# Output stores through two queues, and a finer table of stages for the schedule, in an attention and two-MoE kernel

## The chip, the cores and the metric

The kernel runs on one core of a Trainium2 chip. The metric is the device time of one execution in microseconds (us). TensorE (PE) multiplies matrices, with a sequencer of its own for the loads of the stationary operand (PEld); VectorE (DVE), ScalarE (ACT) and GpSimd (POOL) work on elements; SyncE (SP) issues transfers to the core's 16 DMA engines. Each engine runs its instructions in the order in which the program has them.

## The reference

Three parts follow each other; all data are fp32.

```python
# attention, B4 H8 S768 D64: local window of 96 and 8 global keys, ALiBi bias
a = softmax(where(keep, q @ k.T / 8 - slope * dist, -1e9)); x = a @ v     # -> x (3072, 512)
# first layer, 512 -> 1024 -> 512
h = x @ w_in; s = h * softmax(h); x = layernorm(s) * g_ln @ w_out
# soft MoE: 32 slots, 8 experts of 512 -> 1024 -> 512
logits = x @ phi                                   # (3072, 32)
d = softmax(logits, axis=0); slots = d.T @ x       # over the tokens
slots = relu(slots @ w1[e]) @ w2[e]                # 4 slots for each expert e
out = softmax(logits, axis=1) @ slots              # (3072, 512)
```

The softmax over the tokens and the slot inputs need every token, so nothing of the experts can be computed before the last token tile is through the first layer.

## The kernel before, in words

The 3072 tokens are 24 tiles of 128. For each tile `att_load` (line 555) loads q, k and v, `att_quad` (565) does the attention of four heads, `x_out` (639) makes the tile's x in two parts, and `moe` (649) does the first layer: two groups of twelve 128x512 matmuls, one for each half of the 1024 columns, a maximum of each half on DVE, the exponent of each half on ACT, the product on DVE, and the layernorm. Tiles are taken in pairs by `slots_of` (730): transposes and logits, `l4` (the logits, 32 slots by 256 tokens), matmuls with the constant `sel4` that give the logits by slot and by token, a running maximum and sum by slot, the exponents for the slots (`l4` again) and for the tokens (`c_all`), and the update of `acc`, the weighted sum of the tokens. The last two tiles (22 and 23) are taken singly; tile 23 has its logits from `last_logits` (705) and its layernorm from `bn_stats`. Then `slot_inputs` (811) makes the 32 slot inputs, `hidden` (841, stage `up`) and `slot_outputs` (867, stages `down0` and `down1`) run the experts over 32 weight tiles of 1 MB (`next_wx`, 800), and `combine` (917, stages `out0` and `out1`) makes the output, once for each half of 256 columns: six groups `g4` of four token tiles, each of four matmuls into two PSUM banks, an ACT copy for the first bank, a DVE copy for the second, and one store of 512 KB whose rows in memory are 256 floats (1 KB) long.

Nothing of this is issued in the order of the code. The class `Plan` records every instruction with a stage name, the one that was set last by `self.stage(...)`. `order` (273) sorts them by a list schedule: an instruction's priority is the length of the longest path behind it plus the offset of its stage from the table `AHEAD` (69 to 71); `schedule` (226) takes, from the instructions that can start within `look` ns, the one of highest priority, and lets `PE` keep the shape of its array unless another instruction is ahead by `STAY`. The best of six rounds by the planner's own clock is taken, and `issue` (287 on) writes the instructions out in that order; line 297 stands for all of them in the profile. So the table decides the order on every engine, and each engine then runs in that order.

The buffers' names in the orders and the profile: `b_61` to `b_68` are the PSUM banks b0 to b7, `s_...` parts of the 25 slots in SBUF, `acc`, `c_all`, `l_69` (`l4`), `sel_75` (`sel4`) and `small` as above; a number behind a name is the buffer's. Profile rows leave the numbers out.

Of the kernel before, what the change touches and what calls it, by code (L numbers as in the profile page):

```python
# [57 lines left out]
class Plan:  # L58
# [7 lines left out]
        ("ACT", "ACT"): 130, ("ACT", "DVE"): 140, ("ACT", "PE"): 160, ("ACT", "POOL"): 160,  # L66
        ("POOL", "POOL"): 104, ("POOL", "PE"): 135, ("POOL", "DVE"): 80, ("POOL", "ACT"): 150,
    }
    TURN, STAY, DEEP = 68, 1362, 240
    WRITES = ("out", "accum_out")  # L70
    AHEAD = {"att": -720, "conv": -1209974, "ct": 295072, "down0": 1163900, "down1": -340751, "init": -242959, "load": -1228290, "logits": -521737, "moe": -630, "out0": 2023604, "out1": 496991, "slots": 82, "sums": -2292290, "tab": 2166439, "tail": 2777910, "up": -870817, "w": 865355, "w2": 249441}

    def __init__(self, nc):
        self.nc = nc
# [195 lines left out]
                    waiting[ops[i]["eng"]].append(i)  # L270
        return start, fin, nth

    def order(self, rounds=6, look=121):
        n = len(self.ops)
        pred = [o["pred"] for o in self.ops]
        back = [{} for _ in range(n)]
        for i in range(n):
            for j, lag in pred[i].items():
                back[j][i] = lag
        tail = [0.0] * n  # L280
        for i in reversed(range(n)):
            tail[i] = self.ops[i]["ns"] + max((lag + tail[k] for k, lag in back[i].items()), default=0.0)
        prio = [-x - self.AHEAD.get(o["stage"][0], 0) for x, o in zip(tail, self.ops)]
        best = None
        for _ in range(rounds):
            start, fin, nth = self.schedule(pred, prio, look, True)
            if best is None or max(fin) < best[0]:
                best = (max(fin), start, nth)
            prio = [-x for x in self.schedule(back, [-x for x in fin], look)[1]]
        self.end, start, nth = best  # L290
        return sorted(range(n), key=lambda i: (start[i], nth[i]))
# [28 lines left out]
class Build:  # L320
# [244 lines left out]
    def att_quad(self, t, hq):  # L565

        self.stage("att", t)
        nc = self.nc
        first = t % NQB == 0
        n, m = P if first else WIN, WIN - P  # L570
        x = self.qkv[t]
        v = x[:, 4 * QK:4 * QK + 512]
        pr = self.pr_ring()[:, 0:4 * WIN].rearrange("p (h n) -> p h n", h=4)
        st = self.att_st()
        ps = [self.bank(SC + j) for j in range(2)]
        qk = x[:, 2 * hq * QK:2 * hq * QK + 2 * QK]
        if t < SPLIT:
            parts = [(qk, qk)]
        else:
            hi, lo = f32r(self.qk_ring()), f32r(self.qk_ring())  # L580
            if hq:
                nc.vector.tensor_copy(out=hi, in_=qk)
            else:
                nc.scalar.copy(out=hi, in_=qk)
            nc.gpsimd.tensor_tensor(out=lo, in0=qk, in1=f32v(hi), op=ALU.subtract)
            parts = [(hi, hi), (hi, lo), (lo, hi)]
        for i2 in range(2):
            q = i2 * QK
            with self.together():
                for i, (a, b) in enumerate(parts):  # L590
                    for j in range(2):
                        r = slice(64 * j, 64 * j + 64)
                        nc.tensor.matmul(out=ps[j][:, 256 * i2:256 * i2 + n], lhsT=a[r, q:q + P], rhs=b[r, q + P:q + P + n],
                                         start=(i == 0), stop=(i == len(parts) - 1))
        for h in range(4):
            i2, j = divmod(h, 2)
            nc.vector.tensor_tensor_reduce(
                out=pr[:, h, 0:n], in0=ps[j][:, 256 * i2:256 * i2 + n], in1=self.tabs[first][:, 4 * hq + h, :], scale=-0.125,
                scalar=3.0e38, op0=ALU.add, op1=ALU.min, accum_out=st[:, h:h + 1],
            )  # L600
        for h in range(4):
            nc.scalar.activation(out=pr[:, h, 0:n], in_=pr[:, h, 0:n], func=AF.Exp, bias=st[:, h:h + 1], scale=-1.0,
                                 accum_out=st[:, 8 + 2 * h:9 + 2 * h])
        share = st[:, 4:8]
        nc.vector.tensor_reduce(out=share, in_=st[:, 8:16].rearrange("p (h c) -> p h c", c=2), axis=AX.X, op=ALU.add)
        nc.vector.reciprocal(out=share, in_=share)
        tr = []
        for i2 in range(2):
            w = pr[:, 2 * i2:2 * i2 + 2]
            nc.gpsimd.tensor_tensor(out=w[:, :, 0:n], in0=w[:, :, 0:n],  # L610
                                    in1=share[:, 2 * i2:2 * i2 + 2].unsqueeze(2).to_broadcast([P, 2, n]), op=ALU.mult)
            pt = self.t_ring().rearrange("p (c n) -> p c n", c=4)
            ptT = self.pt_ring().rearrange("p (c n) -> p c n", c=4)
            tr.append(ptT)
            with self.together():
                for j in range(2):
                    nc.tensor.transpose(pt[:, j, :], w[:, j, 0:P], self.ident)
                if not first:
                    for j in range(2):
                        nc.tensor.transpose(pt[0:m, 2 + j, :], w[:, j, P:WIN], self.ident)  # L620
            nc.scalar.copy(out=ptT[:, 0:2, :], in_=pt[:, 0:2, :])
            if not first:
                nc.scalar.copy(out=ptT[0:m, 2:4, :], in_=pt[0:m, 2:4, :])
        av = self.bank(AV).rearrange("p (c n) -> p c n", c=4)
        for i2 in range(2):
            hp, ptT = 2 * hq + i2, tr[i2]
            with self.together():
                for j in range(2):
                    h = 2 * hp + j
                    nc.tensor.matmul(out=av[64 * j:64 * j + 64, hp, :], lhsT=v[:, h * D:(h + 1) * D], rhs=ptT[:, j, :],  # L630
                                     start=True, stop=first)
                if not first:
                    vt = self.vt[t]
                    for j in range(2):
                        h = 2 * hp + j
                        nc.tensor.matmul(out=av[64 * j:64 * j + 64, hp, :], lhsT=vt[0:m, h * D:(h + 1) * D],
                                         rhs=ptT[0:m, 2 + j, :], start=False, stop=True)

    def x_out(self, t):
        nc = self.nc  # L640
        x = self.x_views[t % (2 * NX)]
        xh, xl = f32r(x[:, 0:512]), f32r(x[:, 512:1024])
        av = self.bank(AV)
        nc.scalar.copy(out=xh, in_=av)
        nc.vector.tensor_tensor(out=xl, in0=av, in1=f32v(xh), op=ALU.subtract)
        self.x[t] = (xh, xl)


    def moe(self, u):
# [20 lines left out]
        for half in range(2):  # L670
            o = slice(half * 512, half * 512 + 512)
            nc.scalar.activation(out=ex[:, o], in_=hs[half], func=AF.Exp, bias=st[:, 2:3], scale=1.0,
                                 accum_out=st[:, 4 + half:5 + half])
            nc.vector.scalar_tensor_tensor(out=z[:, o], in0=hs[half], scalar=1.0, in1=ex[:, o], op0=ALU.mult,
                                           op1=ALU.mult, accum_out=st[:, 6 + half:7 + half])
            if last:
                nc.vector.bn_stats(out=self.bn[:, half, :], in_=z[:, o])
        nc.vector.tensor_reduce(out=st[:, 8:10], in_=st[:, 4:8].rearrange("p (a b) -> p a b", a=2), axis=AX.X, op=ALU.add)
        nc.vector.tensor_scalar(out=st[:, 3:4], in0=st[:, 9:10], scalar1=-1.0 / DFF, scalar2=None, op0=ALU.mult)
        scaled, eps = st[:, 10:11], st[:, 12:13]  # L680
# [48 lines left out]

    def slots_of(self, *us):  # L730

        self.stage("slots", us[0])
        nc = self.nc
        k = len(us)
        zs = [self.z.pop(u) for u in us]
# [6 lines left out]
        else:  # L742
            pl = pd = self.ld_bank(us[0])
            by_slot, by_token = pl[:, 256:256 + k * P], pl[:, 0:k * NS].rearrange("p (k s) -> p k s", k=k)
            for i, z in enumerate(zs):
# [8 lines left out]
                with self.together():  # L754
                    for r in range(2):
                        for g in range(4):
                            nc.tensor.matmul(out=pl[32 * g:32 * g + 32, i * P:(i + 1) * P], lhsT=self.w2[:, r * 4 + g, :],
                                             rhs=zt[:, r * 4 + g, :], start=(r == 0), stop=(r == 1), tile_position=(0, 32 * g))
            nc.vector.tensor_copy(out=l4, in_=pl[:, 0:k * P])
            with self.together():  # L760
                nc.tensor.matmul(out=by_slot, lhsT=self.sel4, rhs=l4, start=True, stop=True)
# [22 lines left out]
        with self.together():  # L784
            for i in range(k):
                nc.tensor.transpose(pd[:, 256 + i * P:256 + (i + 1) * P], dT[:, i * P:(i + 1) * P], self.ident)
        nc.vector.tensor_copy(out=d, in_=pd[:, 256:256 + k * P].rearrange("p (k n) -> p k n", k=k)[:, :, 0:NS])
        with self.together():
            for i, z in enumerate(zs):
# [127 lines left out]
    def combine(self, half, sc):  # L917
        nc = self.nc
        self.stage("out%d" % half)
        for g4 in range(6):  # L920
            o = self.o_ring()
            for pair in range(2):
# [6 lines left out]
                    nc.vector.tensor_copy(out=dst, in_=ps)  # L929
                else:  # L930
                    nc.scalar.copy(out=dst, in_=ps)
            nc.sync.dma_start(
                out=self.out[g4 * 512:(g4 + 1) * 512, half * 256:half * 256 + 256].rearrange("(i p) e -> p i e", p=P),
                in_=o.rearrange("p (i e) -> p i e", i=4),
            )
# [291 lines left out]
```

## Time and profile before

| | us |
|---|---|
| median of 3 runs | 434.69 (434.65 to 435.98) |
| profiled execution | 434.6 |
| its span | 432.9 |

| engine | busy us | share | instructions |
|---|---|---|---|
| PE | 396.7 | 92% | 3595 |
| PEld | 294.8 | 68% | 3595 |
| DVE | 321.6 | 74% | 1209 |
| ACT | 308.8 | 71% | 952 |
| POOL | 187.5 | 43% | 180 |

The span runs from the first to the last event of the execution; the time is a little longer, by what lies around it. A share is a mean over stages: PE is full for most of the span, but not at its end. The trace gives, besides, the stretches in which each engine is full, what an engine waited for, and the instructions in order of time.

### The profile page before, as it was taken

Reading aid. Unit: us, or ns where it says so; the run is one execution under the profiler, and the core shown is the slowest. Engines: PE = TensorE matmul, PEld = TensorE weight load, DVE = VectorE, ACT = ScalarE, POOL = GpSimd, SP = SyncE. Lnnn points to the kernel's source line nnn. Section 1 sums busy time; section 2 is a strip of 40 time slices with the busy share of each in tenths; the row PEclk is TensorE's granted clock in tenths of the full one; section 3 lists DMA queues with packets and bytes.
Section 4 is the critical chain, followed back from the end, with each engine's and each line's share of the span. In section 5 each row is a group of like instructions: output and inputs, shape, how many; then the busy total and the mean of one; then the engine's idle time right before and its main releaser. Section 6 shows DMA issues by size and latency. Waiting matters only on the chain.

```text
span 432.9 us, 10268 instructions
## 1 busy us (share of the span) xinstructions
PE 396.7 (92%) x3595; PEld 294.8 (68%) x3595; DVE 321.6 (74%) x1209; ACT 308.8 (71%) x952; POOL 187.5 (43%) x180
## 2 busy tenths in 40 slices
PE   1898999999999999999999999999999998899960
PEld 0555666778888878887887887878877876334540
DVE  6889897989888888888887888987577879301360
ACT  4899999988888788987988788888546555211240
POOL 1679878675563555735555466372100004100000
PEclk9999999999999999999999999999999999999995
DMA  7983767193312332212331213214320599999597
GB/s 280 345 270 126 277 241 246 48 359 137 117 35 84 117 116 95 79 48 109 117 117 48 90 75 118 94 46 188 160 97 2 201 366 338 397 405 423 230 339 227
DMA packets 20139, 78.01 MB, mean 180 GB/s; under 512 B 2480, under 2 KB 8624, under 8 KB 15984
## 3 DMA queue, kind: packets, MB, share of 16 engines
q1 hardware_dynamic: 20080, 77.28, 48.7%
q8 instruction: 30, 0.49, 0.5%
q14 instruction: 29, 0.24, 0.2%
HBM read 70.98 MB, written 6.29 MB: 179 GB/s over the span
## 4 chain that ended last, share of the span: by engine, by line
PE 80%; ACT 6%; DVE 6%; POOL 2%; DMA 2%; issue 1%; SPq 0%; DVEq 0%; POOLq 0%; ACTq 0%
PE b L297 80%; ACT s L297 6%; DVE s L297 3%; DVE small L297 2%; POOL s L297 2%; DMA s<-in_qkv_dram 2%; DVE l L297 1%; SPq L297 0%; DVE acc L297 0%; DVE small L383 0%; DVE small L381 0%; DVE small L382 0%; DVE small L384 0%; DVE small L379 0%; DVEq L297 0%
## 5 line engine op out<-in xcount | busy, mean ns | idle before, releaser
L297 PE MATMUL b<-s,s 128*128 128x512 f32 (+3 forms) x1568 | 235.0, 347 | 2.7 <-DVE s L297 1.8
L297 PEld LDWEIGHTS b<-s,s 128*128 128x128 f32 (+3 forms) x1568 | 149.4, 153 | 42.9 <-issue 11.1
L297 ACT ACTIVATE s<-s,small 128x240 f32<-128x240 f32 (+2 forms) x215 | 117.7, 555 | 13.4 <-DVE small L297 13.3
L297 ACT COPY s<-b 128x256 f32<-128x256 f32 (+1 forms) x244 | 94.9, 438 | 36.2 <-PE b L297 34.6
L297 POOL TENSOR_TENSOR s<-s,s 128x736 fp32r<-128x736 f32 (+2 forms) x56 | 90.2, 1615 | 61.9 <-ACT s L297 30.5
L297 POOL TENSOR_TENSOR s<-s,small 128x480 f32<-128x480 f32 (+1 forms) x96 | 89.7, 954 | 60.6 <-DVE small L297 39.3
L297 PE MATMUL b<-ident,s 128*128 128x128 f32 (+1 forms) x600 | 90.8, 279 | 5.6 <-ACT s L297 3.2
L297 PEld LDWEIGHTS b<-ident,s 128*128 128x128 f32 (+1 forms) x600 | 69.2, 140 | 28.7 <-issue 9.2
L297 DVE TENSOR_SCALAR small<-small 128x1 f32<-128x1 f32 (+2 forms) x289 | 60.1, 215 | 13.4 <-ACT s L297 6.0
L297 DVE CUSTOM_DVE_ANT_0 s<-b,s 128x240 f32<-128x240 f32 (+1 forms) x192 | 64.5, 382 | 4.9 <-PE b L297 4.4
L297 PE MATMUL b<-s 64*128 64x240 f32 (+2 forms) x528 | 52.1, 320 | 11.1 <-DMA s<-in_qkv_dram 9.3
L297 PEld LDWEIGHTS b<-s 64*128 64x128 f32 (+1 forms) x528 | 39.2, 194 | 23.9 <-DMA s<-in_qkv_dram 9.3
L297 DVE TENSOR_REDUCE small<-b 128x1 f32<-128x512 f32 (+3 forms) x73 | 39.0, 557 | 7.1 <-PE b L297 5.7
L297 ACT ACTIVATION_READ_ACCUMULATOR s<-s,small 128x1 f32 x215 | 42.9, 200 | 0.0
L297 ACT ACTIVATE s<-b,small 128x512 f32<-128x512 f32 x49 | 33.5, 689 | 9.3 <-DVE small L297 7.8
L297 DVE SCALAR_TENSOR_TENSOR s<-b,s 128x512 f32<-128x512 f32 x48 | 32.3, 689 | 7.4 <-ACT s L297 4.1
L297 DVE COPY s<-b 128x512 f32<-128x512 f32 (+1 forms) x20 | 12.3, 635 | 23.6 <-PE b L297 23.3
L297 ACT CAST s<-b 128x512 fp32r<-128x512 f32 (+1 forms) x32 | 18.5, 579 | 15.7 <-PE b L297 15.6
L297 PE MATMUL b<-s,l 128*32 128x256 f32 (+1 forms) x320 | 27.4, 469 | 1.2 <-DVE l L297 0.9
L297 POOL CAST s<-c_all 128x256 fp32r<-128x256 f32 x6 | 2.4, 396 | 58.6 <-DVE s L297 55.1
L297 DVE TENSOR_REDUCE small<-small 128x4 f32<-128x8 f32 (+2 forms) x96 | 14.8, 154 | 13.4 <-ACT s L297 12.1
L297 ACT ACTIVATE s<-s 128x512 f32<-128x512 f32 (+1 forms) x32 | 21.3, 691 | 2.8 <-DMA s<-in_w_in_dram 2.8
(82 smaller groups left out, 292.7 us busy)
## 6 DMA issues: line engine op xcount, KB each, us to landing
s<-in_wx_dram SPq DMA_DIRECT2D x32, 1024.0 KB, 7.7
s<-in_qkv_dram SPq DMA_DIRECT2D x24, 992.0 KB, 5.1
out_dram<-s SPq DMA_DIRECT2D x12, 512.0 KB, 5.5
s<-in_v_tail_dram SPq DMA_DIRECT2D x20, 224.0 KB, 5.2
s<-in_w_in_dram SPq DMA_DIRECT2D x8, 512.0 KB, 4.8
s<-in_w_out_dram SPq DMA_DIRECT2D x8, 512.0 KB, 4.0
acc<-in_phi_dram SPq DMA_DIRECT2D x1, 64.0 KB, 4.9
small<-in_n_dram SPq DMA_DIRECT2D x1, 2.0 KB, 2.7
```

Source lines behind the costliest of these rows:

```text
L297: f(*(self.now(x, age) for x in a), **{k: self.now(x, age) for k, x in kw.items()})
```

## The change

The transfers of `combine` go alternately to SP (even `g4`) and POOL (odd `g4`), the table of offsets is new, with more stages in it, and `STAY` and `look` have other values. New stage names split `att` (`qk`, `soft`, `norm`, `turn`, `av`), `x_out` (`x`), the tail of `moe` (`ln`) and `slots_of` (`zt`, `slots`, `dz`). No instruction is added or removed.

```diff
-    TURN, STAY, DEEP = 68, 1362, 240
+    TURN, STAY, DEEP = 68, 1443, 240
-    AHEAD = {"att": -720, "conv": -1209974, "ct": 295072, "down0": 1163900, "down1": -340751, "init": -242959, "load": -1228290, "logits": -521737, "moe": -630, "out0": 2023604, "out1": 496991, "slots": 82, "sums": -2292290, "tab": 2166439, "tail": 2777910, "up": -870817, "w": 865355, "w2": 249441}
+    AHEAD = {"att": 336137, "av": -663, "conv": -1209818, "ct": 563852, "down0": 994095, "down1": -40210, "dz": 431, "init": -12329, "ln": -607, "load": -1228971, "logits": -259756, "moe": -630, "norm": 1317823, "out0": 1889835, "out1": 753347, "qk": -630, "slots": 940, "soft": -623, "sums": -2272370, "tab": 2748248, "tail": 3369283, "turn": -720, "up": -1587723, "w": -142477, "w2": 861412, "x": -746, "zt": 73}
...
-    def order(self, rounds=6, look=121):
+    def order(self, rounds=6, look=122):
...
+        self.stage("qk", t)
         for i2 in range(2):
             q = i2 * QK
...
     def x_out(self, t):
+        self.stage("x", t)
         nc = self.nc
...
     def slots_of(self, *us):
 
-        self.stage("slots", us[0])
+        self.stage("zt", us[0])
...
+            self.stage("slots", us[0])
             nc.vector.tensor_copy(out=l4, in_=pl[:, 0:k * P])
...
+        self.stage("dz", us[0])
         nc.vector.tensor_copy(out=d, in_=pd[:, 256:256 + k * P].rearrange("p (k n) -> p k n", k=k)[:, :, 0:NS])
...
-            nc.sync.dma_start(
+            (nc.gpsimd if g4 % 2 else nc.sync).dma_start(
                 out=self.out[g4 * 512:(g4 + 1) * 512, half * 256:half * 256 + 256].rearrange("(i p) e -> p i e", p=P),
                 in_=o.rearrange("p (i e) -> p i e", i=4),
             )
```

The first place is PE in the first layer of the last tile, around the matmuls into b0 (`b_61`) and b1 (`b_62`); `b_68<-s_82,w_71` and `b_68<-s_100,w_71` are the logits of tiles 20 and 21, `b_68<-l_69,sel_75` and `b_68<-sel_75,l_69` the selection matmuls of these logits.

```order
-L297 MATMUL b_68<-s_82,w_71 32x128 x8
-L297 MATMUL b_68<-s_100,w_71 32x128 x8
 L297 MATMUL b_61<-s_92,s_91 128x512
...
-L297 MATMUL b_68<-l_69,sel_75 128x256
-L297 MATMUL b_68<-sel_75,l_69 128x32 x2
+L297 MATMUL b_68<-s_82,w_71 32x128 x8
+L297 MATMUL b_68<-s_100,w_71 32x128 x8
 L297 MATMUL b_62<-s_92,s_91 128x512
...
+L297 MATMUL b_68<-l_69,sel_75 128x256
+L297 MATMUL b_68<-sel_75,l_69 128x32 x2
```

The logits moved behind the group of b0, and the selection behind the group of b1.

The second place is ACT at the same time: the exponents of the logits (`l_69`, `c_all`), those of the last tile's two halves (`s_100` from `b_61` and `b_62`), and the copies of transposes (`s_82` from `b_67`).

```order
 L297 ACTIVATE l_69,small<-b_68,small 128x256
+L297 COPY s_82<-b_67 128x512
 L297 ACTIVATE c_all,small<-b_68,small 128x32 x2
 L297 ACTIVATE small<-small 128x1
-L297 COPY s_82<-b_67 128x512
 L297 ACTIVATE s_100,small<-b_61,small 128x512
+L297 COPY s_82<-b_67 128x512
 L297 ACTIVATE s_100,small<-b_62,small 128x512
-L297 COPY s_82<-b_67 128x512
```

One copy now stands ahead of the exponents of the token weights, and one between those of the two halves.

The third place is the end of POOL's order, behind its last work on `c_all`.

```order
 L297 CAST s_100<-c_all 128x8x32
 L297 TENSOR_TENSOR s_100<-c_all,s_100 128x8x32
+L297 DMA out_dram<-s_4121 128x4x256
+L297 DMA out_dram<-s_3753 128x4x256
+L297 DMA out_dram<-s_3577 128x4x256
+L297 DMA out_dram<-s_4121 128x4x256
+L297 DMA out_dram<-s_3577 128x4x256
+L297 DMA out_dram<-s_3753 128x4x256
```

Six of the twelve stores left SP for POOL; SP keeps the other six.

## Rows read from the trace of the kernel before

**Rows 1.** The chain of waits: start us, us, what.

```profile
209.85 138.64 PE b L297 x1233
```

**Rows 2.** Busy time by stretch: PE, PEld, DVE, ACT, POOL, clock, DMA share, GB/s.

```profile
88.00:348.00 260.00, 259.96 (x2401) 209.82 (x2401) 213.65 (x859) 206.54 (x654) 117.82 (x99) 1.00 0.31 111
348.00:376.00 28.00, 24.36 (x214) 16.50 (x212) 20.36 (x77) 14.76 (x40) 6.71 (x12) 1.00 0.95 369
376.00:408.00 32.00, 30.43 (x372) 12.80 (x372) 4.16 (x8) 2.76 (x5) 0.00 (x0) 1.00 0.93 383
...
411.00:428.00 17.00, 7.38 (x65) 5.29 (x55) 7.69 (x18) 4.68 (x9) 0.00 (x0) 0.82 1.02 340
428.00:433.00 5.00, 0.00 (x0) 0.00 (x0) 0.00 (x0) 0.00 (x0) 0.00 (x0) 0.50 0.29 87
```

**Rows 3.** Waits of PEld from 88 to 348 us: total us, times, longest us.

```profile
PEld b L297 <- issue: 13.8, 58, 0.4
```

**Rows 4.** Timeline of PE, 346 to 368 us: start, us, what.

```profile
349.22 1.08 PE L297 MATMUL b<-s,w 128*32 128x128 f32 x32
...
353.13 0.59 PE L297 MATMUL b<-l,sel 128*128 128x256 f32 x2
...
353.92 2.99 PE L297 MATMUL b<-s,s 128*128 128x512 f32 x12
...
358.19 1.07 PE L297 MATMUL b<-s,l 128*32 128x256 f32 x16
```

**Rows 5.** Timeline of ACT, 353 to 362 us.

```profile
355.50 0.47 ACT L297 ACTIVATE l<-b,small 128x256 f32<-128x256 f32 x1 [0.65 <-DVE small L297]
355.87 0.20 ACT L297 ACTIVATION_READ_ACCUMULATOR l<-b,small 128x1 f32 x1
...
356.64 0.28 ACT L297 ACTIVATE c_all<-b,small 128x32 f32<-128x32 f32 x1
...
358.29 0.59 ACT L297 COPY s<-b 128x512 f32<-128x512 f32 x1 [0.39 <-PE b L297]
358.77 0.69 ACT L297 ACTIVATE s<-b,small 128x512 f32<-128x512 f32 x1
...
359.45 0.69 ACT L297 ACTIVATE s<-b,small 128x512 f32<-128x512 f32 x1
```

**Rows 6.** Timeline of DVE, 353 to 368 us.

```profile
356.73 0.81 DVE L297 TENSOR_SCALAR s<-s,small 128x1024 f32<-128x1024 f32 x1
...
357.75 0.68 DVE L297 TENSOR_REDUCE small<-b 128x1 f32<-128x512 f32 x1
...
359.32 0.48 DVE L297 SCALAR_TENSOR_TENSOR acc<-acc,small,b 128x256 f32<-128x256 f32 x1 [0.53 <-PE b L297]
...
360.94 0.69 DVE L297 BATCH_NORM_STATS2 small<-s 128x6 f32<-128x512 f32 x1
...
361.74 0.68 DVE L297 BATCH_NORM_STATS2 small<-s 128x6 f32<-128x512 f32 x1
```

**Rows 7.** Timeline of PE, 372 to 420 us.

```profile
376.18 10.51 PE L297 MATMUL b<-s,l 128*32 128x512 f32 x96 [0.38 <-DVE l L297]
...
403.77 1.93 PE L297 MATMUL b<-s,s 128*32 128x256 f32 x32 [0.55 <-DVE l L297]
...
406.27 4.27 PE L297 MATMUL b<-s,s 128*32 128x256 f32 x48
```

**Rows 8.** Timeline of DVE, 405 to 420 us.

```profile
408.67 2.75 DVE L297 COPY s<-b 128x512 f32<-128x512 f32 x4 [1.47 <-PE b L297]
```

**Rows 9.** All stores: issue ns (min/median/max), first and last start us.

```profile
L297 SPq DMA_DIRECT2D out_dram<-s x12: 372/1206/1320, 409.5 to 423.5; - x12
...
DMA to landing us min/median/max: 3.0/5.5/7.8
```

**Rows 10.** The same view from 422.2 us on: the last two stores.

```profile
L297 SPq DMA_DIRECT2D out_dram<-s x2: 1251/1274/1296, 422.1 to 423.5; - x2
...
DMA to landing us min/median/max: 7.6/7.7/7.8
```

**Rows 11.** The page's costliest groups: POOL, busy us and mean ns of one.

```profile
L297 POOL TENSOR_TENSOR s<-s,s 128x736 fp32r<-128x736 f32 (+2 forms) x56 | 90.2, 1615 | 61.9 <-ACT s L297 30.5
```

**Rows 12.** Busy time by stretch, one microsecond of the weight loads.

```profile
398.00:399.00 1.00, 1.00 (x24) 0.65 (x20) 0.00 (x0) 0.00 (x0) 0.00 (x0) 1.00 1.04 434
```

More of the change, by code (lines that the diff above doesn't have):

```diff
@@ L594, in att_quad @@
                                          start=(i == 0), stop=(i == len(parts) - 1))
+        self.stage("soft", t)
         for h in range(4):
@@ L608, in att_quad @@
         for i2 in range(2):
+            self.stage("norm", t)
             w = pr[:, 2 * i2:2 * i2 + 2]
@@ L611, in att_quad @@
                                     in1=share[:, 2 * i2:2 * i2 + 2].unsqueeze(2).to_broadcast([P, 2, n]), op=ALU.mult)
+            self.stage("turn", t)
             pt = self.t_ring().rearrange("p (c n) -> p c n", c=4)
@@ L623, in att_quad @@
                 nc.scalar.copy(out=ptT[0:m, 2:4, :], in_=pt[0:m, 2:4, :])
+        self.stage("av", t)
         av = self.bank(AV).rearrange("p (c n) -> p c n", c=4)
@@ L677, in moe @@
                 nc.vector.bn_stats(out=self.bn[:, half, :], in_=z[:, o])
+        self.stage("ln", u)
         nc.vector.tensor_reduce(out=st[:, 8:10], in_=st[:, 4:8].rearrange("p (a b) -> p a b", a=2), axis=AX.X, op=ALU.add)
```

## The prediction

> **What bounds the kernel now.** I read the chain of waits first, then the busy times by stretch, then the timelines of the stretches in which no engine is full. The chain says that the end hangs on TensorE (PE): one piece of it alone, from 209.85 us, runs 138.64 us without a break [rows 1]. The table of stretches says where that holds and where it does not [rows 2]. From 88 to 348 us PE is busy 259.96 of 260.00 us. From 348 to 376 us it is busy 24.36 of 28.00 and no engine is full: here the last two token tiles must be finished before the slot inputs, and so the matmuls of the second layer, can start; this is a chain of small steps over PE, VectorE (DVE) and ScalarE (ACT). From 376 to 408 us PE is busy again (30.43 of 32.00). From 411 to 428 us PE is busy 7.38 of 17.00, while the 16 DMA engines have a busy share of 1.02 and move 340 GB/s: the stores of the output. After 428 us no engine works; the last store lands. So a change of order can win only what little PE loses in the long stretch, or in the hand-off (348 to 376), or by an earlier first store; a change of queue only in the last 24 us. Up to about 88 us all five engines have the same order in both kernels, so that stretch counts as unchanged.
>
> **The order from 88 to 348 us.** PE runs the same matmuls in both kernels there, in another sequence. Between them PE loses time only where it waits, and the waits of the weight loads (PEld), which run under the queued matmuls, are small: 13.8 us in 58 waits that nothing releases, that is 13.8 / 58 = 0.24 us each, the longest 0.4 us [rows 3]. These 58 go with changes of the array's shape (a matmul with other rows or columns than the one before). Counted in the two orders, the stretch has 112 such changes before and 110 after. If each costs the whole 0.24, the gain is 0.5 us; if the matmuls already queued hide them, it is 0. I take **-0.2 us**. A PE that idles 0.04 us in 260 leaves nothing else to win, but a new order could bring a new wait: up to +1 us is kept for the range.
>
> **The hand-off, 348 to 376 us.** The last tile's first layer is two groups of twelve 128x512 matmuls, into banks b0 and b1. Before, the logits of tiles 20 and 21 run ahead of b0 (349.22), the selection matmuls of these logits between b0 and b1 (353.13 to 353.92), and b1 starts at 353.92 [rows 4]. After, the logits (1.08 us) stand between the groups and the selection behind both. So b1 starts at 353.92 - 0.79 = 353.1 and its end comes 0.8 us sooner, but the selection starts at about 356.0 instead of 353.13, 2.9 us later.
>
> What needs both is on ACT. Before, the exponent of the 32 slots (`l4`), at 355.50, the two of the token weights (0.28 us each) and a tiny one were done by 357.9, and only a copy of 0.59 stood ahead of the exponent of b0, which starts at 358.77; that of b1 follows at once, at 359.45 [rows 5]. After, all of these come after the late selection. It is done at about 356.0 + 0.6; the maximum over 256 columns (0.4 us, since 512 columns take 0.68 [rows 6]) and one tiny DVE step of 0.2, with the gaps between engines, bring the slot exponent to 357.5. On ACT then follow, from start to start, 0.57 (0.37 to the reading of its sum at 355.87, and 0.2 for that), a copy 0.48 (358.29 to 358.77), two exponents of 0.28 and 0.15 for the tiny one: 357.5 + 1.76 = 359.26, **+0.5 us** against 358.77. The earlier b1 does not help, for its DVE maximum can be done by 358.2, ahead of that. Then a copy now stands between the exponents of b0 and b1: another **+0.5**. On DVE the first half's statistics, 0.6 us from 360.94 to the next start, now come ahead of b1's product instead of behind it: **-0.6**; the update of `acc` (0.48, about 0.4 from start to start) moves behind them, in front of b1's product: **+0.4**. So the second statistics end about 0.8 us later than 362.4 (361.74 + 0.68). What follows up to the first matmul of the second layer has the same members in both: **+0.8 us**. Bounds: the copy and the five steps may overlap better than I place them, and then b1's 0.8 us sooner comes through (-0.8); or a transpose of tile 22, which now runs later, holds the copy between the exponents, and b1's half pays once more (+1.9: the 0.8 and the 1.07 of the sixteen 32x256 matmuls of tile 22 that run at 358.19, behind which such a transpose may stand [rows 4]).
>
> **376 to 411 us.** The second layer's matmuls keep their order but for eight 32x256 matmuls of the first `down` half, which now fill the 0.55 us in which PE waits for a DVE copy at 403.77; they were behind it, in the row of 48 at 406.27 [rows 7]. These eight take 0.5 us (4.27 / 48 each would be 0.7), so the first matmul of the output comes 0.5 us sooner, less what the copies of the first output tile wait: I take **-0.4 us** for the first store. The first DVE copy of the output started at 408.67 and four take 2.75 us, 0.69 each [rows 8]. Nothing else of weight moves; the loads of weights in this stretch land ahead of their use.
>
> **The stores.** Twelve stores of 512 KB: SyncE (SP) issues the first at 409.5 and the last at 423.5; an issue takes 0.37 us at the least and 1.2 at the median. A store lands 3.0 us after its issue when the queue is empty, 7.6 for the last two: 423.5 + 7.6 = 431.1 [rows 9, 10]. The issue gets slow because the engines are full, not the other way round: 12 x 0.524 = 6.29 MB at 340 GB/s are 18.5 us, and 412.5 (409.5 + 3.0) + 18.5 = 431.0 is just when the last lands. After, SP issues six and GpSimd (POOL) six. Both queues go to the same full engines, so I put the drain at **0**.
>
> What POOL pays for an issue has no row here. POOL has finished its other work by then (no POOL instruction after 376 us), so nothing is behind it. Bounds from the nearest rows: 0.37 us (SP with an empty queue) and 1.6 us (POOL's own costliest step, 1615 ns [rows 11]); nearest is SP's median, 1.2, the same work on another queue. With p us per issue the last POOL store lands at about 410 + 6p + 3.0 (the second store is ready one copy after the first). That is later than 431.1 only from p = 3.0 on. At 1.2 it is 420 and hidden.
>
> One thing speaks against POOL here. DVE copies of 128x512 out of PSUM run until 420 us, 0.69 us each, 1.3 ns a column; a DVE step from SBUF to SBUF ran 1024 columns in 0.81 us, 0.8 ns a column [rows 6, 8], so the copies of the output do not run in the faster way. If a copy nevertheless held each POOL issue for its 0.69, six would cost 4.1 us spread over the stores, p = 1.9, still hidden. The Trainium skill (SBUF — State Buffer, "SBUF: two separate sides") says that a DMA from GpSimd's queue has its descriptors written by the GpSimd cores, and that these are locked out while VectorE runs an instruction that takes both ports; it gives some 3.1 us instead of 0.62 for such a transfer, and by that the last POOL store would land at 410 + 18.6 + 3.0 = 431.6 and the sum would be 0.5 us more. By the rows the rule does not apply, since these copies read PSUM at the slow rate.
>
> **The sum.** The profiled execution took 434.6 us, 432.9 of it the span; it lies 0.1 under the median of the runs, 434.69. -0.2 + 0.8 - 0.4 + 0 = +0.2: **434.8 us**. A measurement of this kernel tells about 0.3% from no change, 1.3 us, so this is no change; with the bounds of the small terms the case covers 434.0 to 435.9.
>
> **The rivals.**
> *Hand-off slips (slower).* The ACT copy between the two exponents waits for a late transpose: +1.9 in place of +0.8, and no PE gain: 434.6 + 1.9 - 0.4 = 436.1. For it: ACT is a queue in fixed order, and the b1 exponent now stands behind that copy. Against: the transposes of tile 22 are put ahead of their use.
> *POOL's issue decides (slower).* It is one price, p per store on POOL, and decides from p = 3.0 us. At 3.5 the last lands at 410 + 21 + 3 = 434, 2.9 us later: 434.8 + 2.9 = 437.7. For it: the price is not known, and each issue describes 512 rows of 1 KB. Against: POOL is otherwise idle, and both bounds lie far below.
> *Two queues drain faster (faster).* The loads reached 434 GB/s in full flow [rows 12], the stores 340. If the gap is that of one queue, 6.29 MB at 420 GB/s take 15.0 us, 3.5 less: 434.8 - 3.5 = 431.3. Against: the engines are at a busy share of 1.02 already, so it is the 1 KB rows that cost.
> *The hand-off gains (faster).* b1's 0.8 us come through to the end: 434.6 - 0.2 - 0.8 - 0.4 = 433.2.
> *The queue change does nothing at all* is the forecast itself.
>
> **How the numbers follow.** Forecast 0.47; hand-off slips 0.15; POOL decides 0.12; faster drain 0.11; hand-off gains 0.15. Faster by over 0.3% (under 433.4) are the drain and the gain: 0.26. Slower by over 0.3% (over 436.0) are the slip and POOL: 0.27. The rest, 0.47, is within 0.3%. The range leaves out the faster drain (0.11) and the dear part of POOL's price (0.09): 433.0 to 437.0.
>
> **What would show it.** Right: 110 or so short waits and PE full to 348 us; the first matmul of the second layer 0.6 us later than 376.18; the first store at 409.5 + 0.2 = 409.7; stores at 340 GB/s; POOL's issues under 3 us each. Wrong: a rate of the stores well over 340 GB/s or a last landing more than 1 us from 431; a start of the second layer before 375.5 or after 377.5; POOL issues of 3 us or more.

## The result and the profile after

The changed kernel takes 438.0 us (median of 16 executions, 435.85 to 440.36) against 434.69 (434.39 to 436.03, also 16): a ratio of 1.0062, 95% interval 1.0047 to 1.0078. It is slower, by 0.6%, where no change was forecast: 3.2 us above the forecast 434.8 and above the upper end of the range, 437.0. The executions of one kernel lie in steps of about 1.5 us, each with a lower mean granted clock of TensorE: before has 434.4 to 434.7 (12 of 16) and 435.8 to 436.0 (4), the changed kernel 435.9 to 436.4 (4 of 16), 437.0 to 438.1 (6) and 439.1 to 440.4 (6), and an execution of the lowest step is called undisturbed here. The profiled execution took 439.12 us, 437.3 of it the span; it is of the third step.

The busy times by stretch of the changed kernel, then single microseconds of it (PE, PEld, DVE, ACT, POOL, clock, DMA share, GB/s; against [rows 2]):

```profile
88.00:348.00 260.00, 259.84 (x2405) 209.72 (x2403) 212.24 (x859) 207.30 (x654) 118.76 (x99) 1.00 0.31 111
348.00:376.00 28.00, 24.30 (x206) 15.98 (x198) 20.60 (x76) 13.14 (x39) 7.03 (x12) 0.94 0.88 353
376.00:408.00 32.00, 30.25 (x342) 12.99 (x346) 3.90 (x7) 2.85 (x5) 0.00 (x0) 0.95 0.97 390
...
371.00:372.00 1.00, 0.64 (x3) 0.52 (x4) 0.31 (x1) 0.41 (x1) 0.72 (x1) 0.63 1.01 426
372.00:373.00 1.00, 1.00 (x9) 0.67 (x11) 0.84 (x4) 0.06 (x1) 0.00 (x0) 0.50 1.02 434
...
378.00:379.00 1.00, 1.00 (x8) 0.34 (x12) 0.00 (x0) 0.00 (x0) 0.00 (x0) 0.54 0.99 385
379.00:380.00 1.00, 1.00 (x8) 0.22 (x4) 0.00 (x0) 0.00 (x0) 0.00 (x0) 0.50 0.95 369
```

The long stretch is as before. In the two behind it the granted clock is no longer 1.00: it falls to 0.50, the lower level (1.2 GHz), at 371 us and again at 378 us. What that costs, and the gaps of PE ahead of it, stand in the timeline of PE of the changed kernel (against [rows 4, 7]):

```profile
358.47 0.66 PE L297 MATMUL b<-ident,s 128*128 128x128 f32 x4 [1.13 <-ACT s L297]
...
359.78 1.07 PE L297 MATMUL b<-s,l 128*32 128x256 f32 x16 [0.32 <-DVE l L297]
...
368.81 0.63 PE L297 MATMUL b<-ident,s 128*128 128x128 f32 x4 [0.50 <-ACT s L297]
...
370.12 0.64 PE L297 MATMUL b<-s,l 128*32 128x256 f32 x8 [0.36 <-DVE l L297]
371.36 0.69 PE L297 MATMUL b<-ident,acc 128*128 128x128 f32 x2 [0.60 <-DVE acc L297]
...
372.83 2.81 PE L297 MATMUL b<-s,w 128*32 128x512 f32 x16
376.51 1.08 PE L297 MATMUL b<-sel,s 128*128 128x32 f32 x8 [0.87 <-ACT s L297]
377.97 12.20 PE L297 MATMUL b<-s,l 128*32 128x512 f32 x96 [0.38 <-DVE l L297]
...
424.34 0.63 PE L297 MATMUL b<-s 128*128 128x256 f32 x3 [2.45 <-ACT s L297]
```

Before, the same sixteen matmuls took 1.92 us and the 96 took 10.51 [rows 7], and the longest gaps from 357 to 378 us were 0.53 and 0.81 us:

```profile
365.90 0.64 PE L297 MATMUL b<-s,l 128*32 128x256 f32 x8 [0.53 <-DVE l L297]
...
371.98 1.92 PE L297 MATMUL b<-s,w 128*32 128x512 f32 x16
374.71 1.08 PE L297 MATMUL b<-sel,s 128*128 128x32 f32 x8 [0.81 <-ACT s L297]
```

So the clock costs 0.9 + 1.7 = 2.6 us in these two rows. The last row of the changed kernel is a new wait, and it is not the clock's. The timelines of its DVE (with a row of the hand-off that is needed below) and of its ACT name the cause:

```profile
362.55 0.68 DVE L297 BATCH_NORM_STATS2 small<-s 128x6 f32<-128x512 f32 x1
...
423.72 0.69 DVE L297 COPY s<-b 128x512 f32<-128x512 f32 x1 [1.68 <-DMA out_dram<-s]
```

```profile
423.70 1.07 ACT L297 COPY s<-b 128x512 f32<-128x512 f32 x2 [2.62 <-DMA out_dram<-s]
```

Copies of the second half wait for a store to land. The output goes through six buffers, so the group `g4 = 3` of the second half writes where that of the first half was, and must wait until that has left. The stores by queue (issue ns, first and last start), then the one store that is waited for:

```profile
L297 SPq DMA_DIRECT2D out_dram<-s x6: 372/384/410, 412.4 to 424.8; - x6
L297 POOL DMA_DIRECT2D out_dram<-s x6: 752/753/933, 413.6 to 426.2; - x6
...
DMA to landing us min/median/max: 3.0/5.5/8.9
```

```profile
L297 POOL DMA_DIRECT2D out_dram<-s x1: 754/754/754, 418.0 to 418.0; - x1
...
  ACT s L297: 2.6, 1
  DVE s L297: 1.7, 1
...
DMA to landing us min/median/max: 5.6/5.6/5.6
```

That store is issued at 418.0 and lands at 418.0 + 5.6 = 423.6; before, the last store of the first half was issued at 414.4 and landed at 414.4 + 5.9 = 420.3. The first store is 412.4 - 409.5 = 2.9 us late, the last one is issued at 426.2 and lands 8.9 us later, at 435.1 instead of 431.1.

### The profile page after: what moved, and what is told of

Read it like the earlier page. It is cut to its first block, busy times and chain, and to the rows that moved or that the text cites. A ratio compares the mean times of both kernels' runs of the same rounds, so it can differ in the third digit from the quotient of the medians.

```text
span 437.3 us, 10271 instructions
## 1 busy us (share of the span) xinstructions
PE 399.5 (91%) x3595; PEld 295.7 (68%) x3595; DVE 320.6 (73%) x1209; ACT 308.5 (71%) x952; POOL 193.5 (44%) x186
## 3 DMA queue, kind: packets, MB, share of 16 engines
HBM read 70.98 MB, written 6.29 MB: 177 GB/s over the span
## 4 chain that ended last, share of the span: by engine, by line
PE 77%; ACT 6%; DVE 6%; DMA 3%; POOL 2%; issue 2%; SPq 0%; ACTq 0%; POOLq 0%; DVEq 0%
PE b L297 77%; ACT s L297 6%; DVE s L297 3%; DVE small L297 3%; POOL s L297 2%; DMA s<-in_qkv_dram 2%; DMA out_dram<-s 1%; DVE acc L297 0%; POOL out_dram L297 0%; SPq L297 0%; DVE l L297 0%; ACT l L297 0%; ACT c_all L297 0%; ACTq L297 0%; POOLq L297 0%
## 5 line engine op out<-in xcount | busy, mean ns | idle before, releaser
L297 PE MATMUL b<-s,s 128*128 128x512 f32 (+4 forms) x1568 | 235.8, 347 | 2.1 <-DVE s L297 1.8
L297 PEld LDWEIGHTS b<-s,s 128*128 128x128 f32 (+3 forms) x1568 | 149.5, 153 | 41.9 <-issue 12.1
L297 ACT COPY s<-b 128x256 f32<-128x256 f32 (+2 forms) x244 | 95.7, 438 | 37.3 <-PE b L297 33.2
L297 POOL TENSOR_TENSOR s<-s,small 128x480 f32<-128x480 f32 (+1 forms) x96 | 90.8, 966 | 60.2 <-DVE small L297 30.3
L297 PE MATMUL b<-ident,s 128*128 128x128 f32 (+1 forms) x600 | 92.0, 280 | 6.9 <-ACT s L297 4.3
L297 DVE TENSOR_REDUCE small<-b 128x1 f32<-128x512 f32 (+2 forms) x73 | 39.0, 557 | 7.8 <-PE b L297 6.5
L297 PE MATMUL b<-s,l 128*32 128x256 f32 (+1 forms) x320 | 29.1, 492 | 1.1 <-DVE l L297 1.1
L297 POOL DMA_DIRECT2D out_dram<-s x6 | 4.7, 783 | 50.5 <-DVE s L297 42.6
```

What stands on the lines that cost most here:

```text
L297: f(*(self.now(x, age) for x in a), **{k: self.now(x, age) for k, x in kw.items()})
```

## The experiments

Twelve kernels follow, with 11 or 12 executions each (the last one 6). In all of them the order of every engine is written out by the planner from one of the two tables, as in before or as in the changed kernel, so that one thing can be changed with every other instruction where it was. The helper `planned` sorts with one table and gives the order; the queue of the stores is chosen apart from it. The edits are shown in part, against the changed kernel. On the chips of these runs, before had a median of 435.7 to 435.95, since more of its executions were at about 436.1; its undisturbed ones were at 434.6 there too.

**Queue alone.** The order of before; odd stores through POOL.

```diff
-        for i in self.order():
+        chosen, _ = self.planned("before", False)
...
+            queue = real.gpsimd if g4 % 2 else real.sync
```

> The order of every engine is that of the kernel before; only the odd stores go through POOL. Theory 1 (the time is lost in three places: the hand-off about 0.8 us, a TensorE clock that falls to half around 371 to 382 us in some executions, and a late first store with the tail behind it): within 1 us of before, 434.3 to 435.7, granted clock 1.00 from 348 to 408, POOL issues of 0.75 us, last landing 431 to 432. Rival (the second queue itself costs): 437 to 438, with a last store that lands 8 us or more after its issue.

Measured: 437.43 us against 435.95, ratio 1.0033 (1.0015 to 1.0051); the 434.3 to 435.7 of Theory 1 were missed. Undisturbed executions are at 435.8 to 436.5, so the queue costs 1.2 us or more where nothing else differs. The stretch of this run in which the DMA engines are full, then its stores:

```profile
413.00:430.00 17.00, 7.12 (x59) 5.17 (x51) 7.54 (x18) 4.77 (x9) 4.18 (x6) 0.85 1.01 332
```

```profile
L333 SPq DMA_DIRECT2D out_dram<-s x6: 372/397/579, 411.3 to 422.2; - x6
L333 POOL DMA_DIRECT2D out_dram<-s x6: 752/753/933, 412.5 to 423.7; - x6
...
DMA to landing us min/median/max: 3.0/6.2/12.1
```

332 GB/s instead of 340 [rows 2]: 6.29 MB take 18.95 us instead of 18.5. The last store of SP, issued at 422.2, lands 12.1 us later; before, no store took more than 7.8 [rows 9]. In the packets of the trace, the first and the last data packet of the stores are 21.5 us apart, against 20.3 before. POOL's packets hold 4 KB and take 0.20 us each, SP's hold 1 KB and take 0.05: four of them cost about one of POOL's. The rival stood half right: the queue costs, but not all of it. (Nor was the clock 1.00, as Theory 1 had it: this execution, in before's order, had a half-clock stretch at 377 us.)

**Order alone.** The order of the changed kernel, all stores through SP.

```diff
-        for i in self.order():
+        chosen, _ = self.planned("after", True)
...
+            queue = real.sync
```

> The order of the changed kernel, all twelve stores through SP. Theory 1: 436.5 to 438, with executions spread over 3 us or more as the changed kernel's are, since the half clock comes from the order. Rival (the second queue itself costs): 434.5 to 435.7, executions as close together as those of before.

Measured: 438.61 us (435.74 to 439.87), ratio 1.0062 (1.0039 to 1.0084): with SP alone as slow as the change, and 0.6 us over what Theory 1 gives. The busy times by stretch of this run show the stores back at before's rate, and the clock at half in other microseconds:

```profile
413.00:430.00 17.00, 6.87 (x50) 4.90 (x49) 7.65 (x17) 4.77 (x9) 0.00 (x0) 0.85 1.02 339
...
360.00:361.00 1.00, 1.00 (x12) 0.51 (x16) 0.96 (x3) 1.00 (x3) 0.33 (x1) 0.56 1.01 418
361.00:362.00 1.00, 1.00 (x10) 0.35 (x3) 0.56 (x2) 0.03 (x1) 0.79 (x2) 0.50 1.10 459
```

Here the half clock came at 360 us, behind the gap of 1.13 us on PE. From the first to the last data packet it is 20.3 us, as before. So Theory 1 holds for the clock (the executions spread over 4 us), and a second loss must lie in the order: the one undisturbed execution is at 435.74, 1.1 us over before's 434.6.

**TensorE's gaps filled.** The changed kernel, both queues, with 30 transposes of the identity added in the gaps.

```diff
+        FILL = {2670: (8, 2), 2622: (2, 2), 2721: (4, 1), 2730: (3, 1), 2732: (4, 1), 2786: (6, 1), 2788: (3, 1)}
...
+            for _ in range(FILL.get(last, (0, 0))[0]):
+                t = self.fill[FILL[last][1]]
+                self.nc.tensor.transpose(t, self.fill[0], self.fill[0])
```

`FILL` says behind which step, how many, and into which bank.

> The changed kernel with 30 transposes of the identity added on TensorE, in the gaps of the hand-off, into banks that are free there. Theory 1: the granted clock stays at 1.00 from 348 to 408 us, the spread of the executions shrinks to under 1.5 us, 436.0 (435.3 to 436.5). Rival (the second queue, or the longer hand-off, costs and the clock is a side effect): 437.5 to 438.5.

Measured: 436.24 us (436.12 to 437.49), ratio 1.003 (1.0016 to 1.0043). With more instructions it is 1.8 us under the changed kernel's median, ten of twelve executions within 0.4 us. Its busy times by stretch:

```profile
348.00:376.00 28.00, 27.04 (x241) 19.05 (x234) 20.65 (x76) 13.59 (x39) 7.03 (x12) 1.00 0.91 363
376.00:408.00 32.00, 31.12 (x379) 13.45 (x379) 4.33 (x8) 2.76 (x5) 0.00 (x0) 1.00 0.93 384
...
411.00:428.00 17.00, 7.43 (x57) 5.47 (x53) 8.04 (x18) 4.77 (x9) 4.28 (x6) 0.84 1.01 332
```

The clock stays at 1.00 to 408 us in this execution, and the first store goes at 409.4, where before's went at 409.5. What is left, 1.6 us, is behind that point. Two of the twelve executions are still a step higher (437.4 and 437.5).

**Front of before, tail of the change**, POOL included.

```diff
+        g1, a1 = self.planned("before", False)
+        g2, a2 = self.planned("after", True)
+        late = {"up", "down0", "down1", "out0", "out1"}
```

The stages of `late`, and the loads of their weights, stand in the order of the second table, all others in that of the first.

> The order of before up to the first matmul of the second layer, from there that of the changed kernel, with its six stores on POOL. Theory 1: first layer and hand-off as before, clock 1.00, so 434.3 to 436.0: what remains is the late g4 = 3 store of the first half (issued behind a copy of the second down stage) and its effect on the last landing. Rival (the tail costs all of it): 437 to 438.

Measured: 436.95 us, ratio 1.0025 (1.001 to 1.004); undisturbed 435.7 to 435.95. With before's front the executions a step higher are as frequent as in before on the same chip (7 of 12 here, at 436.8 or more, 19 of 33 there), so the extra ones of the change come from its front, and about 1.2 us from its tail.

**Before with its own gaps filled**: 22 transposes, all stores through SP.

> The kernel before with 22 transposes of the identity added on TensorE in the gaps of the hand-off, all stores through SP. If gaps on TensorE are what lets the clock fall: no half-clock stretch from 348 to 408 us, nearly all executions at 434.6 (434.3 to 434.9), so the median of this chip's kernel before, 435.9, is beaten by about 1.3 us. Rival (the clock falls by chance, whatever the gaps): the executions divide between 434.6 and 436.1 as those of before do.

Measured: 434.67 us (434.35 to 435.02) against 435.91 on the same chip, ratio 0.9982 (0.9969 to 0.9994). All twelve executions are undisturbed, where 16 of 29 of before were not. The rival, chance, is out. Its busy times by stretch:

```profile
348.00:376.00 28.00, 26.76 (x238) 18.50 (x236) 20.24 (x77) 14.74 (x40) 6.69 (x12) 1.00 0.96 372
376.00:408.00 32.00, 30.60 (x373) 12.84 (x374) 4.04 (x7) 2.76 (x5) 0.00 (x0) 1.00 0.93 377
```

**Order of the change, gaps filled, all stores through SP.**

> The order of the changed kernel, the 30 added transposes, and all stores through SP: the two suspected losses are both taken away. Theory 1: what is left is the new order alone, first store 0.1 us sooner than before's undisturbed 409.5, from first to last data packet of the stores 20.3 us, time 434.4 to 435.2. Rival (the longer hand-off of the new order costs by itself): 435.5 or more.

Measured: 436.01 us (435.58 to 437.08), ratio 1.0009 (0.9996 to 1.0022). The rival's number, 435.5 or more, came out: with gaps filled and the queue put right the order still loses 1.3 us against 434.67. Its cause, the hand-off, did not: the timeline of ACT says where the loss is:

```profile
421.08 1.07 ACT L339 COPY s<-b 128x512 f32<-128x512 f32 x2 [2.79 <-DMA out_dram<-s]
```

It is the wait for a landing again, with SP alone. That gave Theory 2, that the tail's order and the six buffers cost, and not the hand-off. Four runs test it.

**Front of before (22 transposes), tail of the change, SP alone.**

> The order of before with the 22 added transposes up to the first matmul of the second layer, from there the changed kernel's order, all stores through SP. Theory 2 (the new tail costs by itself: the g4 = 3 store of the first half goes late, the second half's copies into its buffer wait for its landing, so the last copies, the last store and the end-of-program branch come 1 to 2 us later): 435.5 to 436.0 against 434.67 of the same kernel with before's tail. Rival (the new front costs): 434.5 to 434.9.

Measured: 435.57 us (435.35 to 436.9). Against 434.67 with before's tail the new tail costs 0.9 us, and the timeline of ACT has the same wait:

```profile
420.21 1.07 ACT L360 COPY s<-b 128x512 f32<-128x512 f32 x2 [2.82 <-DMA out_dram<-s]
```

**Front of the change (30 transposes), tail of before, SP alone.**

> The changed kernel's order with the 30 added transposes up to the first matmul of the second layer, from there the order of before, all stores through SP. Theory 2: 434.3 to 434.8, so the new front costs nothing when the clock does not fall. Rival (the longer hand-off costs by itself): 435.4 or more.

Measured: 434.94 us (434.71 to 435.23), just over the expected 434.8: at full clock the new front costs 0.3 us over before's.

**Twelve output buffers instead of six**, otherwise the run above with the changed order, 30 transposes and SP; the order of every engine is the same, since the planner sorts with six buffers and only the kernel itself runs with `buffers` at twelve.

```diff
-        self.o_ring = Ring(self.part(W_SLOTS[11 + i // 2], (i % 2) * 1024, 1024) for i in range(6))
+        self.o_ring = Ring(self.part(W_SLOTS[11 + (i // 2) % 3 - 3 * (i // 6)], (i % 2) * 1024, 1024) for i in range(self.buffers))
```

> As the run with the changed kernel's order, 30 added transposes and all stores through SP (435.85), but the output goes through twelve buffers instead of six, so no copy of the second half waits for a store to land; the order of every engine is the same. Theory 2: the waits of ACT and DVE for the store's landing (2.6 us) and TensorE's gap behind them go, last copy at about 421, 434.4 to 434.9. Rival (the order of the last matmuls costs by itself, or the drain of the stores sets the end): 435.6 to 436.0.

Measured: 434.85 us (434.47 to 436.47) instead of 436.01. The timeline of ACT shows no wait for a landing, and the last copy starts at 418.9 (three executions, at 436.1 to 436.5, are a step higher):

```profile
416.14 2.54 ACT L339 COPY s<-b 128x512 f32<-128x512 f32 x5 [1.29 <-PE b L339]
418.91 0.58 ACT L339 COPY s<-b 128x512 f32<-128x512 f32 x1 [0.22 <-PE b L339]
```

So it is the wait, and neither the order of the last matmuls nor the drain of the stores.

**Only the first ten of the 30 transposes**, changed order, SP alone.

> The changed kernel's order, all stores through SP, and only the first ten of the 30 transposes (in the gap of 1.13 us after the first transposes of tile 22 and the 0.32 us behind it). If the early gap alone brings the extra half-clock stretches of the new order: executions like those with before's front, none or one stretch, 435.8 to 437.3, none at 438.5 or above. Rival (the later gaps bring them): up to two stretches remain, median 437 to 438.6.

Measured: 437.62 us (435.67 to 439.25), ratio 1.0045 (1.0024 to 1.0067). Three of eleven executions are still at 439: the rival. With all 30 none of 12 was that high. So the early gap of 1.13 us is not the only one that counts; those between 367 and 378 us do too. Which of them was not tried.

**Odd stores through ACT's queue**, order of before.

> The order of before, the odd stores through ACT's queue in place of POOL's. If two queues of any kind stretch the drain of the stores: 21.3 us from first to last data packet, as with POOL. If it is POOL's own descriptors (packets of 4 KB, 0.20 us each): packets of 1 KB and 20.3 us, as with SP alone; ACT then loses at most 1.3 us per issue in front of its own copies, so 434.6 to 436.5.

Measured: 436.39 us, ratio 1.0027 (1.0011 to 1.0043), undisturbed 436.1 to 436.5. The packets are of 1 KB and the time is inside the second side's bounds, but the span fits neither: from first to last data packet it is 19.4 us, shorter than with SP alone. With the engines full they move 342 GB/s (411 to 416 us) and 335 (419 to 430), as with SP alone, so the loss of 1.5 us or more is not in the drain. The DMA queues of this run from 405 us on (q10 is ACT's: packets, MB, share of the engines' time):

```profile
q1 hardware_dynamic: 3227, 3.48, 30.9%
q10 hardware_dynamic: 3168, 3.15, 28.3%
```

But the copies now wait for landings by more than 2 us; with before's order and SP alone the longest such wait in a profile was 0.7 us. Who waited for its stores, in us and times:

```profile
  ACT s L333: 2.6, 1
  DVE s L333: 2.2, 1
```

In the trace the store that they waited for was issued late and landed fast: its issue stands in ACT's own order, behind a cast and copies, so it went at 418.2, where before's last store of the first half went at 414.4, and it landed in 4.4 us, where that one took 5.9. So this run does not separate the queue from the late issue, and a cost of two queues as such is not shown by it.

**All twelve stores through POOL**, order of before.

> The order of before, all twelve stores through POOL. If the packets of POOL's queue are the cost: 1536 packets of 4 KB at 0.20 us on 16 engines are 19.2 us of transfer, against 18.9 with 1 KB packets, so from first to last packet 20.7 at least, and 0.5 to 1.5 us more than before's undisturbed 434.6. If mixing two queues is the cost: 20.3 us or less and 434.3 to 434.9 undisturbed.

Measured: 438.62 us, ratio 1.007 (1.005 to 1.0089), more than expected: the profiled execution, 438.5, has a granted clock of 1.00 from 348 to 408 us, so the queue alone costs 3.9 us here, where 0.5 to 1.5 were expected. The rate is the lowest of all, the shortest landing takes 3.6 us instead of 3.0, the longest 11.0, and 22.0 us lie between first and last data packet. The stretch of full DMA engines in this run, then its stores:

```profile
412.00:429.00 17.00, 6.76 (x51) 4.93 (x49) 7.28 (x17) 4.86 (x9) 7.30 (x10) 0.83 1.00 323
```

```profile
L333 POOL DMA_DIRECT2D out_dram<-s x12: 752/752/931, 410.1 to 423.9; - x12
...
DMA to landing us min/median/max: 3.6/7.0/11.0
```

So mixing isn't the only cost; POOL's queue is the slower one by itself. Of the 3.9 us, 1.7 are the longer drain (22.0 against 20.3) and 1.2 a later first packet (411.64 against 410.45); the rest lies behind the last one.

## Why the prediction was wrong, step by step

*The order from 88 to 348 us, -0.2.* PE is busy 259.84 of 260.00 us: nothing was won or lost that could be seen. Right within its bounds.

*The hand-off, +0.8.* The second statistics end at 362.55 + 0.68 = 363.23 instead of 362.42: +0.8, as worked out, but in part by luck. The rows of the changed kernel (ACT, ACT, DVE):

```profile
358.94 0.70 ACT L297 ACTIVATE s<-b,small 128x512 f32<-128x512 f32 x1
...
360.07 0.73 ACT L297 ACTIVATE s<-b,small 128x512 f32<-128x512 f32 x1
...
362.34 0.29 DVE L297 COPY l<-b 128x128 f32<-128x128 f32 x1 [0.16 <-PE b L297]
```

The exponent of b0 starts 0.2 us later than before and not 0.5, that of b1 0.6 and not 1.0; from there to the second statistics it is 362.55 - 360.07 = 2.48 us against 361.74 - 359.45 = 2.29, so DVE's part is +0.2 (with the copy shown waiting for PE) and not -0.2. Two errors of 0.4 cancel. With the gaps filled the second layer's first matmul starts at 376.65, 0.5 us later than before. The step that failed is what this hand-off does besides. I took PE's clock as given and wrote that what follows "has the same members in both". The members are the same, but PE now waits 1.13 us at 357 us and 0.3 to 0.9 us six times more from there to 378 us, where before's longest gaps were 0.81 and 0.53. In the profiled execution the clock then runs at 1.2 GHz in two stretches, which cost 2.6 us, and 12 of 16 executions are one or two steps above the lowest. No rival had it. That gaps and not chance bring the steps is shown by the kernels with filled gaps: with before's tail 0 of 24 executions are a step higher (of before itself 16 of 29 on one chip), with the changed tail 8 of 48, all of them by one step. Why those 8 remain is open. The Trainium skill (TensorE: Matmul & The Clock Gate, "A second HAM failure mode: psum-queue depth-cycling") tells of a kernel in which PE idles briefly, but often enough between groups of matmuls that the clock swings between its two levels; the rows here agree, with gaps of 1.13 us and less.

*The first store, -0.4.* From the second layer's first matmul (+1.8 us) to the first store (+2.9) the clock alone adds 1.7, so the eight moved matmuls gave 1.8 + 1.7 - 2.9 = 0.6. With the gaps filled the first store goes at 409.4 against my 409.7. Right.

*"Nothing else of weight moves."* Wrong. The order of DVE showed that the copy of `g4 = 3` had moved behind the copy of the second `down` stage; I read the order of stores as not bound and did not follow the buffer into the second half. Its store is now the last of that half (`s_3577` in the third place of the change; 5.6 us after the first store, where before's last was 4.9 after it), while the copies of the second half still take `g4 = 3` ahead of `g4 = 5`. So its landing holds two engines with further copies behind it, where in before's order only the last copies wait, by 0.7 us at most; the tail's order costs 0.9 us by itself (435.57 against 434.67).

*The stores, 0.* Wrong by 1.0 to 1.2 us. POOL's issue takes 0.75 us (0.93 the first), inside my bounds, far under the 3.0 from which it would decide, and hidden: that rival is out. Two of its issues, at 421.4 and 425.0, lie beside VectorE copies out of PSUM and took 0.75 like the others, so the reading that these copies do not block holds. The Trainium skill (SBUF — State Buffer, "SBUF: two separate sides") gives some 3.1 us instead of 0.62 for a transfer from GpSimd's queue beside a VectorE copy that locks GpSimd out; no issue of POOL here took over 0.93. What I had wrong is that the drain does not depend on the queue. With POOL's queue it is slower (332 GB/s mixed, 323 POOL alone, 336 to 340 SP alone), and a single store lands later (up to 12.1 us mixed and 11.0 POOL alone, against 7.8 before). The faster drain of the rival (420 GB/s) did not come either: the engines were full at 340, as argued against it.

*The sum.* Undisturbed, the queue costs 1.2 us or more alone, the order 1.1 to 1.3 alone, and both together 1.3 to 1.7 (435.9 to 436.4 against 434.6): they overlap. I read this as both making the same last stores late; no run shows it apart. The half clock adds 1.5 us per step: one step at the median gives 438.0. The forecast of "no change" held a hand-off that was right in its sum, and left out three terms: clock, buffer wait, drain.

Left open are which of the later gaps lets the clock fall, why some executions of the changed tail are a step higher with the gaps filled, and why the last store of SP lands 12 us after its issue when POOL's stores share the engines.

## What to carry to other kernels

A new order that leaves PE's work the same can still cost by its gaps: list PE's gaps in a latency-bound hand-off before and after, and look whether the granted clock stays at 1.00; a few dummy transposes into a free bank buy it back (before with 22 of them: ratio 0.9982, the lowest median of these runs). When a store moves to another queue, or later in an order, follow its buffer to the next writer, because the landing, not the issue, sets it free; and look in whose order the issue then stands, for behind ACT's copies it went 3.8 us later. A second queue did not widen full DMA engines here; POOL's narrowed them, from 340 to 332 GB/s.

## What the runs showed of the hardware that was not expected

The end of the program can wait for something other than the stores. After its last work each engine passes a branch before its last instructions. The waits of SP's queue there, before and then in the changed kernel:

```profile
SPq L1165 <- SPq L1165: 4.8, 2, 4.5
```

```profile
SPq L1174 <- SPq L1174: 7.2, 1, 7.2
```

SP sits 7.2 us at that branch instead of 4.5 and runs on at 435.1, just when the last store lands; before, it ran on at 430.7, ahead of the last landing at 431.1. The branch comes behind DVE's last copies (SP waits 1.4 us for DVE ahead of it in the changed kernel), so what delays these delays the branch. That it can set the end by itself is seen where the last store has landed before SP runs on. With the changed tail and SP alone (wait of 6.0 us at the branch) the last store lands at 431.4, SP runs on at 432.0 and the span ends at 433.9; with before's tail it lands at 430.8, SP runs on at 430.6 and the span ends at 432.6. With odd stores on ACT's queue the last landing is at 432.2, SP runs on at 432.9 and the span ends at 434.8. So late copies cost twice: they delay the last store, and the branch behind them.

What the engines wait for there is a reading: in the DMA records of the changed kernel, among the stores, stand packets of 8 and 16 KB of two queues of the kind `instruction`:

```profile
q8 instruction: 4, 0.07, 0.9%
q14 instruction: 8, 0.07, 0.6%
```

Five of them start at 432.3 to 432.5, some 4.3 us behind the branch at 428.0, when the stores have nearly left the engines. I take them for the instructions behind the branch, held up by the stores; no run shows this apart.
